# Few changes of the array's form: padded and stacked 64-row operands, values beside scores, and half of the masks on GpSimd, in a top-k attention with a low-rank mixer

## The chip, the core and the metric

The kernel runs on one core of a Trainium2 chip. The core has a matrix engine (TensorE, PE in the profile; its weight loads are shown apart as PEld), a vector engine (VectorE, DVE), an activation engine (ScalarE, ACT), GpSimd (POOL) and SyncE (SP), which here issues the loads. Each works through its own queue of instructions in order; semaphores hold an instruction until what it needs is there. Data lie in SBUF (128 partitions); PE writes to PSUM, from which ACT or DVE copy the results.

The metric is the device time of one execution in microseconds (us), as the median of several runs. A profile is one execution, with every instruction's start and duration.

## The reference

Eight batches of eight heads, 576 positions, 64 features a head. Attention keeps the 32 largest scores of each row; the heads are joined to 512 channels, mixed over the positions by two low-rank factors (rank 32), and passed through an MLP (512 to 2048 to 512). The parameters come as float64.

```python
def _attn_ref(q, k, v) -> np.ndarray:
    B, H, S, D = q.shape
    top_k = 32
    scale = 1.0 / np.sqrt(D)
    scores = scale * np.matmul(q, k.transpose(0, 1, 3, 2))
    kth = np.partition(scores, -top_k, axis=-1)[..., -top_k:-top_k + 1]
    mask = scores >= kth
    scores = np.where(mask, scores, -1000000000.0)
    scores = scores - np.max(scores, axis=-1, keepdims=True)
    attn = np.exp(scores)
    attn = attn / (np.sum(attn, axis=-1, keepdims=True) + 1e-09)
    return np.matmul(attn, v).astype(np.float32)
...
def _moe_ref(x, U, V, w_ch1, w_ch2) -> np.ndarray:
    xt = x.transpose(0, 2, 1)
    h = xt @ U @ V
    u = x + h.transpose(0, 2, 1)
    ch = np.maximum(u @ w_ch1, 0.0) @ w_ch2
    return (u + ch).astype(np.float32)
```

## The kernel before

**Tiling.** The heads go in pairs; one pair of one batch is a *group*, 32 in all. The 576 positions are four blocks of 128 and a tail of 64, so a group has five *steps*. In steps `t` = 0 to 3 DVE works on two tiles of 128 rows by 576 scores, one for each head (two *chunks*); in the last, `t == NT`, on one tile in which the 64 tail rows of both heads lie one above the other. The profile shows the matrix engine's form as rows*columns: `128*128` is the full array; `64*128` has two halves of 64 rows that work side by side (scores, where a head has 64 features); `128*64` and `64*64` have column halves (values: one head to each half of the result). A float32 product is recorded as two passes, a transpose as one.

**One step on DVE.** `front` calls `select`: four times MAX8 (L253, the eight largest), with three MATCH_REPLACE8 between (L262, which takes those eight out), so that the last of the 32 maxima is the threshold. ACT computes the exponentials (L258, with the negative maximum from L257) meanwhile. Then DVE's `scalar_tensor_tensor` (L265) zeroes what lies under the threshold and sums the row into `den`.

**One step on PE.** PE's order is as written by hand; the other engines' instructions are put in order by a scheduler. Step `n` of the loop (L472) issues, in PE's order: the scores of step `n + 1` (L229, copied by ACT at L239 or L242); MLP work; `back` of step `n - 1`, that is the transposes of its masked exponentials E (L300, 128 columns at a time, a part of 64 last, copied by ACT at L301) and at once the product with the values (L307, result `O`, copied at L316 to `XT`); then a piece of `prep` of the next group (transposes of q and k, L207 and L212). In the last step of a group `front` also adds 1e-9 to `den`, takes the reciprocal (L282, L283), and POOL scales E by it (L284).

**Mixing.** When a group's five steps are through, `mixed` transposes `XT` back (L329, L338), DVE scales it by `den` to `X` (L331), and PE makes the two low-rank products (L345, L357), adding `X` by a product with the identity (L360). After every fourth group a batch's `u` is ready, and `mlp` is put on the list of fillers.

**Filling.** `fill` is called between the pieces of a step. A call advances the mixing of a group by one piece, then adds `share` to an account, `due`, and issues MLP work (L382, L400) while the account is above zero. `share` is made so that a batch's MLP takes 160 calls, eight in each of 20 steps. In a two-head step `back` has four pieces, in the last step of a group three, so that step has seven calls.

**Parameters.** In the first 25 steps or so `next_param` loads one or two blocks a step and rounds them from float64 with ACT (L126, L129), POOL (L127, L138) and DVE (L131, L134).

**Buffers.** q and k have two buffers, the score tiles (`Ssb`) three, E six single tiles, PT two, the values three. The PSUM pool of the transposes, `O` and the mixing has two buffers, that of the MLP two, that of the scores two.

Of the kernel before, what the change touches and what calls it, by code (L numbers as in the profile page):

```python
# [21 lines left out]
def kernel(  # L22
# [25 lines left out]

    nc = tc.nc
# [18 lines left out]
    loads = ctx.enter_context(tc.tile_pool(name="loads", bufs=2))  # L68
# [16 lines left out]
    vas = [const.tile([P, 2, NT + 1, D], F32, name=f"va{i}") for i in range(NV)]  # L85
# [56 lines left out]
    def same(a):  # L142
# [5 lines left out]
        ([moe_U[MAIN:S, :]], [(U[0:TAIL, NT, :], same)]),  # L148
# [23 lines left out]
    probs = {}  # L172

    def load(g):
        b, h0 = g // NPAIR, 2 * (g % NPAIR)
        tiles = []
        for name, src in (("q", q), ("k", k)):
            t = loads.tile([P, NT + 1, 2, D], F32, tag=f"ld_{name}", name=f"ld_{name}")
            for i in range(2):
                nc.sync.dma_start(  # L180
                    t[:, 0:NT, i, :],
                    src[b, h0 + i, 0:MAIN, :].rearrange("(p t) d -> p t d", t=NT),
                )
            nc.sync.dma_start(
                t[0:TAIL, NT, :, :], src[b, h0 : h0 + 2, MAIN:S, :].rearrange("h p d -> p h d")
            )
            tiles.append(t)
        va = vas[g % NV]
        for i in range(2):
            nc.sync.dma_start(  # L190
                va[:, i, 0:NT, :],
                v[b, h0 + i, 0:MAIN, :].rearrange("(p t) d -> p t d", t=NT),
            )
        nc.sync.dma_start(
            va[0:TAIL, :, NT, :], v[b, h0 : h0 + 2, MAIN:S, :].rearrange("h p d -> p h d")
        )
        raw[g] = tiles

    def prep(g):

        tiles = raw.pop(g)
# [9 lines left out]
        for i, t in enumerate(tiles):  # L211
            nc.tensor.transpose(  # L212
                tp[:, i, :],
                t[0:TAIL, NT].rearrange("p h d -> p (h d)"),
                ident[0:TAIL, 0:TAIL],
            )
# [3 lines left out]
    def scores(g, t):  # L220
# [4 lines left out]
        S2 = attn.tile([P, 2, S], F32, tag="Ssb", name="Ssb", bufs=3)  # L225
# [10 lines left out]
        for i, sc in enumerate(scs):  # L236
            cs = slice(i * HALF, (i + 1) * HALF)
            if t < NT:
                nc.scalar.copy(S2[:, :, cs], sc[:, :, 0:HALF])  # L239
            else:  # L240
                for h in range(2):
                    nc.scalar.copy(S2[half(h), 0, cs], sc[half(h), h, 0:HALF])  # L242
        S2s[g, t] = [S2[:, 0], S2[:, 1]] if t < NT else [S2[:, 0]]

    def select(chunks, sums):


        Es = [attn.tile([P, S], F32, tag="E", name="E", bufs=6) for _ in chunks]
# [15 lines left out]
        for c in range(len(chunks)):  # L264
            nc.vector.scalar_tensor_tensor(  # L265
                out=Es[c],
                in0=chunks[c],
                scalar=ms[c][:, 7:8],
                in1=Es[c],
                op0=ALU.is_ge,  # L270
                op1=ALU.mult,
                accum_out=sums[c],
            )
        return Es

    def front(g, t):
# [3 lines left out]
        Es = select(chunks, [den[:, 2 * t + h : 2 * t + h + 1] for h in range(len(chunks))])  # L280
        if t == NT:
            nc.vector.tensor_scalar_add(den, den, 1e-9)  # L282
            nc.vector.reciprocal(den, den)  # L283
            nc.gpsimd.tensor_scalar(Es[0], Es[0], den[:, 2 * NT :], None, ALU.mult)  # L284
            del qkTs[g]
        probs[g, t] = Es

    def back(g, t):

        Es, va = probs.pop((g, t)), vas[g % NV]  # L290
        nh = len(Es)
        PT = attn.tile([P, NT + 1, 2, P], F32, tag="PT", name="PT")
        per = 4 // nh
        for j0 in range(0, NT + 1, per):
            js = range(j0, min(j0 + per, NT + 1))
            n = rows(js[0])
            tp = ps_t.tile([P, per, nh, P], F32, tag="tp", name="tp")
            for j in js:
                for h, E in enumerate(Es):
                    nc.tensor.transpose(tp[0 : rows(j), j - j0, h, :], E[:, cols(j)], ident)  # L300
            nc.scalar.copy(PT[0:n, j0 : js[-1] + 1, 0:nh, :], tp[0:n, 0 : len(js)])  # L301
            yield
        m = rows(t)
        O = ps_t.tile([P, P], F32, tag="tp", name="O")
        for j in range(NT + 1):
            for h in range(2):
                nc.tensor.matmul(  # L307
                    O[half(h), 0:m],
                    lhsT=va[0 : rows(j), h, j, :],
                    rhs=PT[0 : rows(j), j, h, :] if nh == 2 else PT[0 : rows(j), j, 0, half(h)],  # L310
                    start=(j == 0),
                    stop=(j == NT),
                )
        if t == 0:
            XTs[g] = attn.tile([P, S], F32, tag="XT", name="XT")
        nc.scalar.copy(XTs[g][:, cols(t)], O[:, 0:m])  # L316
        yield


    def mixed(g):  # L320
# [5 lines left out]
        X = mlpp.tile([P, NT + 1, P], F32, tag="X", name="X")  # L326
# [10 lines left out]
        tp = ps_t.tile([P, P], F32, tag="tp", name="tp")  # L337
        nc.tensor.transpose(tp[0:TAIL, :], XT[:, cols(NT)], ident)  # L338
        nc.scalar.copy(X[0:TAIL, NT, :], tp[0:TAIL, :])
# [3 lines left out]
        for t in range(NT + 1):  # L343
# [3 lines left out]
                lhsT=U[0 : rows(t), t, :],  # L347
                rhs=X[0 : rows(t), t, :],
# [6 lines left out]
        for chunks, (lo, hi) in zip(PARTS, SPAN):  # L355
            up = ps_t.tile([P, WIDE], F32, tag="tp", name="up")
            nc.tensor.matmul(up[:, 0 : hi - lo], lhsT=Tb, rhs=V[:, lo:hi], start=True, stop=False)  # L357
            for t in chunks:
                n = rows(t)
# [167 lines left out]
```

## Time and profile before

| what | us |
|---|---|
| median of 3 runs | 2040.4 (2039.09 to 2041.24) |
| the profiled execution | 2039.95 |
| its span, first to last instruction | 2038.2 |
| ACT busy | 943.8 |
| MAX8, L253 (1152) | 822.2 |
| MATCH_REPLACE8, L262 (864) | 639.2 |
| mask and sum, L265 (288) | 225.0 |
| MLP passes, L382 and L400 (4096) | 1092.2 |
| scores, L229 | 217.4 |
| transposes of E, L300 | 234.1 |
| values, L307 | 234.9 |

Busy times are the union of a group's instructions; matmuls overlap, so that the times of PE's lines say less than the distances between starts. An idle time in a line is the engine's wait just before, with what ended it.

### The profile page before, as it was taken

To read this page: it belongs to the slowest core of one execution; us is meant where nothing else is said; L and a number is where in the kernel's file an instruction comes from. 1 tells how busy PE (TensorE), PEld (TensorE's weight loads), DVE (VectorE), ACT (ScalarE), POOL (GpSimd) and SP (SyncE) were. 2 spreads that over 40 slices of the span, in tenths; PEclk is the share of its full clock that TensorE was granted. 3 is DMA by queue.
4 is the path that set the end of the run, shared out by engine and by line. 5 is a ranking of instruction groups with operands and counts; after the bars stand their busy time and mean duration, and the time that the engine had idled before them with its cause. 6 is when DMAs were issued, how large, how long until landed. Compare 5 with 4: busy or idle time off the path is not lost.

```text
span 2038.2 us, 30289 instructions
## 1 busy us (share of the span) xinstructions
PE 1861.8 (91%) x11424; PEld 1347.3 (66%) x11424; DVE 1740.4 (85%) x3689; ACT 943.8 (46%) x2217; POOL 166.7 (8%) x137
## 2 busy tenths in 40 slices
PE   5666688999999999999999999999999999999998
PEld 3443355677666776677766776667766776667777
DVE  7999999999998999999999999999999999994000
ACT  4555555454544545454544545454554545443111
POOL 2333232000000000000000000000000000000000
PEclk7666689999999999999999999999999999999999
DMA  3222211010001010010000001010000000000000
GB/s 98 69 70 69 74 52 56 18 32 18 23 18 30 8 29 18 19 31 19 27 14 18 22 16 29 18 31 18 28 13 19 19 19 28 1 14 1 11 14 11
DMA packets 98673, 57.21 MB, mean 28 GB/s; under 512 B 83552, under 2 KB 92000, under 8 KB 98528
## 3 DMA queue, kind: packets, MB, share of 16 engines
q1 hardware_dynamic: 95840, 45.85, 8.6%
q0 software_dynamic: 2688, 9.44, 1.2%
q8 instruction: 90, 1.47, 0.3%
q14 instruction: 55, 0.45, 0.1%
HBM read 45.83 MB, written 9.44 MB: 27 GB/s over the span
## 4 chain that ended last, share of the span: by engine, by line
PE 42%; DVE 34%; issue 13%; ACT 7%; DMA 1%; POOL 1%; SPq 1%; POOLq 0%; DVEq 0%; ACTq 0%
DVE m L253 15%; DVE rr L262 14%; PE mm L400 13%; PE mm L382 10%; PE O L307 7%; PE sc L229 5%; DVE E L265 4%; PE tp L300 3%; ACT E L258 2%; ACT PT L301 2%; ACT Ssb L239 2%; DMA raw<-in_moe_w_ch_dram 1%; PE tp L207 1%; PE up L357 1%; PE up L360 1%
## 5 line engine op out<-in xcount | busy, mean ns | idle before, releaser
L253 DVE MAX8 m<-rr 128x8 f32<-128x576 f32 x864 | 615.9, 748 | 2.8
L382 PE MATMUL mm<-uT,w 128*128 128x256 f32 (+1 forms) x2048 | 547.7, 414 | 3.7 <-ACT hT L392 3.7
L400 PE MATMUL mm<-hT,w 128*128 128x256 f32 (+1 forms) x2048 | 544.5, 412 | 0.0
L382 PEld LDWEIGHTS mm<-uT,w 128*128 128x128 f32 x2048 | 374.0, 191 | 122.4 <-issue 32.1
L400 PEld LDWEIGHTS mm<-hT,w 128*128 128x128 f32 x2048 | 372.5, 190 | 115.0 <-issue 29.9
L262 DVE MATCH_REPLACE8 rr<-m,rr 128x576 f32<-128x576 f32 x576 | 427.3, 742 | 0.0
L300 PE MATMUL tp<-ident,E 128*128 128x128 f32 (+1 forms) x1440 | 234.1, 292 | 98.8 <-DVE E L265 54.5
L300 PEld LDWEIGHTS tp<-ident,E 128*128 128x128 f32 (+1 forms) x1440 | 172.5, 142 | 161.3 <-issue 54.6
L253 DVE MAX8 m<-Ssb 128x8 f32<-128x576 f32 x288 | 206.3, 750 | 83.6 <-ACT Ssb L239 80.3
L307 PE MATMUL O<-PT,va 128*64 128x128 f32 (+3 forms) x3200 | 234.9, 286 | 41.7 <-ACT PT L301 38.5
L307 PEld LDWEIGHTS O<-PT,va 128*64 128x64 f32 (+1 forms) x3200 | 170.5, 144 | 118.5 <-ACT PT L301 59.8
L301 ACT COPY PT<-tp 128x512 f32<-128x512 f32 (+1 forms) x448 | 209.2, 496 | 54.2 <-PE tp L300 51.6
L265 DVE SCALAR_TENSOR_TENSOR E<-Ssb,m,E 128x576 f32<-128x576 f32 x288 | 225.0, 813 | 3.2
L258 ACT ACTIVATE E<-Ssb,nmax 128x576 f32<-128x576 f32 x288 | 223.5, 776 | 8.4
L229 PE MATMUL sc<-qkT 64*128 64x288 f32 (+1 forms) x1280 | 217.4, 457 | 1.6 <-ACT Ssb L239 1.6
L392 ACT ACTIVATE hT<-mm 128x320 f32<-128x320 f32 (+1 forms) x256 | 103.7, 406 | 240.9 <-PE mm L382 239.7
L262 DVE MATCH_REPLACE8 rr<-m,Ssb 128x576 f32<-128x576 f32 x288 | 211.9, 742 | 0.0
L239 ACT COPY Ssb<-sc 128x576 f32<-128x576 f32 x256 | 153.0, 641 | 91.3 <-PE sc L229 89.5
L229 PEld LDWEIGHTS sc<-qkT 64*128 64x128 f32 (+1 forms) x1280 | 112.9, 189 | 67.8 <-issue 40.6
L413 DVE TENSOR_TENSOR oT<-uT,mm 128x320 f32<-128x320 f32 (+1 forms) x64 | 28.4, 444 | 150.8 <-PE mm L400 150.6
L257 ACT ACTIVATE nmax<-m 128x1 f32<-128x1 f32 x288 | 57.4, 199 | 200.5 <-DVE m L253 200.4
L284 POOL TENSOR_SCALAR E<-E,den 128x576 f32<-128x576 f32 x32 | 55.4, 1730 | 1122.6 <-DVE den L283 900.9
(53 smaller groups left out, 947.4 us busy)
## 6 DMA issues: line engine op xcount, KB each, us to landing
raw<-in_moe_w_ch_dram SPq DMA_DIRECT2D x32, 512.0 KB, 3.8
ld_q<-in_q_dram SPq DMA_DIRECT2D x64, 128.0 KB, 2.8
ld_k<-in_k_dram SPq DMA_DIRECT2D x64, 128.0 KB, 2.8
va<-in_v_dram SPq DMA_DIRECT2D x64, 128.0 KB, 2.1
out_dram<-ob POOLq DMA_DIRECT2D x16, 512.0 KB, 3.0
ld_q<-in_q_dram SPq DMA_DIRECT2D x32, 32.0 KB, 2.4
ld_k<-in_k_dram SPq DMA_DIRECT2D x32, 32.0 KB, 2.5
va<-in_v_dram SPq DMA_DIRECT2D x32, 32.0 KB, 2.2
```

The lines of the kernel that those rows point to most:

```text
L229: nc.tensor.matmul(sc[slice(0, n) if t < NT else half(h), h, 0:HALF], lhsT=qkT[half(h), 0, cols(t)], rhs=qkT[half(h), 1, i * HALF : (i + 1 ...
L239: nc.scalar.copy(S2[:, :, cs], sc[:, :, 0:HALF])
L253: nc.vector.max(m, curs[c])
L258: nc.scalar.activation(Es[c], chunks[c], AF.Exp, bias=nmax, scale=SCALE)
L262: nc.vector.match_replace(nxt, ms[c], curs[c], NEG)
L265: nc.vector.scalar_tensor_tensor(out=Es[c], in0=chunks[c], scalar=ms[c][:, 7:8], in1=Es[c], op0=ALU.is_ge, op1=ALU.mult, accum_out=sums[c],)
L300: nc.tensor.transpose(tp[0 : rows(j), j - j0, h, :], E[:, cols(j)], ident)
L301: nc.scalar.copy(PT[0:n, j0 : js[-1] + 1, 0:nh, :], tp[0:n, 0 : len(js)])
L307: nc.tensor.matmul(O[half(h), 0:m], lhsT=va[0 : rows(j), h, j, :], rhs=PT[0 : rows(j), j, h, :] if nh == 2 else PT[0 : rows(j), j, 0, half ...
L382: nc.tensor.matmul(ph[:, 0:w], lhsT=w1[:, cc, f * P : (f + 1) * P], rhs=uT[:, cc, lo:hi], start=(cc == 0), stop=(cc == NC - 1),)
L392: nc.scalar.activation(hTs[f][:, 0:w], ph[:, 0:w], AF.Relu)
L400: nc.tensor.matmul(po[:, 0:w], lhsT=w2[:, f, c * P : (c + 1) * P], rhs=hTs[f][:, 0:w], start=(f == 0), stop=(f == NF - 1),)
```

## The change

The tail operands lose their own forms. The two heads' tail rows of q and k are loaded into one tile, `ends`, and transposed once. The tail columns of both heads' E lie side by side, so that one full transpose turns them; the tail values lie on the diagonal of a tile `vd` (zeros elsewhere), so that one full product serves both heads and starts the sum. In the last step of a group the values are one product of the full array for each block (`vt` has zeros above the tail rows), with the result's rows as positions, scaled by `den` on ACT into `X`'s tail; `XT` has no tail to turn back. The tails of `U` and `X` are stacked or padded to 128 rows as well.

`back` is split. `turns` of step `n - 1` (transposes) stays in step `n`; `values` is issued a step later, for `n - 2`, and the scores of `n + 1` right behind it. Every step has eight calls of `fill`, and the loop has one step more.

Of each two-head step the second head's mask is made by POOL (a comparison written over the scores, and a product) with the sum by ACT; in the first four groups all masks are. q and k have one buffer.

```diff
+    ident2 = const.tile([P, TAIL], F32, name="ident2")
+    nc.gpsimd.tensor_tensor(ident2, ident[:, 0:TAIL], ident[:, TAIL:P], ALU.add)
+    vas = [const.tile([P, 2, NT, D], F32, name=f"va{i}") for i in range(NV)]
+    vds = [const.tile([P, P], F32, name=f"vd{i}") for i in range(NV)]
+    vts = [const.tile([P, 2, D], F32, name=f"vt{i}") for i in range(NV)]
+    xs = [const.tile([P, NT + 1, P], F32, name=f"x{i}") for i in range(2)]
...
-    loads = ctx.enter_context(tc.tile_pool(name="loads", bufs=2))
+    loads = ctx.enter_context(tc.tile_pool(name="loads", bufs=1))
...
-        ([moe_U[MAIN:S, :]], [(U[0:TAIL, NT, :], same)]),
+        ([moe_U[MAIN:S, :]] * 2, [(U[:, NT, :], same)]),
...
 def load(g):
+        ends = loads.tile([P, 2, D], F32, tag="ld_ends", name="ld_ends")
...
+                ends[half(len(tiles))], src[b, h0 : h0 + 2, MAIN:S, :].rearrange("h p d -> p h d")
...
+            nc.sync.dma_start(vd[half(i), half(i)], v[b, h0 + i, MAIN:S, :])
+        nc.sync.dma_start(vt[TAIL:P], v[b, h0 : h0 + 2, MAIN:S, :].rearrange("h p d -> p h d"))
...
 def prep(g):
+        nc.tensor.transpose(
+            tp.rearrange("p i n -> p (i n)"), ends.rearrange("p h d -> p (h d)"), ident
+        )
...
 def scores(g, t):
+        main = S2.rearrange("p (h n) -> p h n", h=2)
+        last = S2[:, MAIN : MAIN + 2 * TAIL].rearrange("p (h n) -> p h n", h=2)
+        nc.scalar.copy(main[:, :, 0:HALF], scs[0][:, :, 0:HALF])
+        nc.scalar.copy(main[:, :, HALF:MAIN], scs[1][:, :, 0 : MAIN - HALF])
+        nc.scalar.copy(last, scs[1][:, :, MAIN - HALF : HALF])
...
 def select(chunks, Es, sums, pools):
+            kth = ms[c][:, 7:8]
+            if pools[c]:
+                nc.gpsimd.tensor_scalar(chunks[c], chunks[c], kth, None, ALU.is_ge)
+                nc.gpsimd.tensor_tensor(Es[c], Es[c], chunks[c], ALU.mult)
+                nc.scalar.activation(chunks[c], Es[c], AF.Copy, accum_out=sums[c])
+            else:
+                nc.vector.scalar_tensor_tensor(
...
 def front(g, t):
+        E2 = attn.tile([P, 2 * S], F32, tag="E", name="E", bufs=3)
+        pools = [g < NPAIR or c == 1 for c in range(n)]
...
-            nc.vector.tensor_scalar_add(den, den, 1e-9)
-            nc.vector.reciprocal(den, den)
-            nc.gpsimd.tensor_scalar(Es[0], Es[0], den[:, 2 * NT :], None, ALU.mult)
...
-    def back(g, t):
+    def turns(g, t):
+        E2 = probs.pop((g, t))
+        nh = 2 if t < NT else 1
+        PT = attn.tile([P, 2 * NT + 1, P], F32, tag="PT", name="PT")
+        PTs[g, t] = PT
+        for h in range(nh):
+            tp = ps_t.tile([P, NT, P], F32, tag="tp", name="tp")
+            for j in range(NT):
+                a = h * (S + TAIL) + j * P
+                nc.tensor.transpose(tp[:, j, :], E2[:, a : a + P], ident)
+            nc.scalar.copy(PT[:, NT * h : NT * h + NT], tp)
             yield
+        tp = ps_t.tile([P, P], F32, tag="tp", name="tp")
+        a = MAIN if nh == 2 else S - P
+        nc.tensor.transpose(tp, E2[:, a : a + P], ident)
+        nc.scalar.copy(PT[:, NT * nh], tp)
+        yield
+
+    def values(g, t):
+        PT = PTs.pop((g, t))
+        va, vd, vt = (a[g % NV] for a in (vas, vds, vts))
         O = ps_t.tile([P, P], F32, tag="tp", name="O")
+        if t == NT:
+            den, x = dens[g], xs[g % 2]
+            with tc.high_priority():
+                nc.vector.tensor_scalar_add(den, den, 1e-9)
+                nc.vector.reciprocal(den, den)
+            for j in range(NT + 1):
+                nc.tensor.matmul(
+                    O,
+                    lhsT=PT[:, j],
+                    rhs=va[:, :, j, :] if j < NT else vt,
+                    start=(j == 0),
+                    stop=(j == NT),
+                )
+            for h in range(2):
+                nc.scalar.mul(x[half(h), NT, half(h)], O[half(h), half(h)], den[half(h), 2 * NT :])
+            return
+        nc.tensor.matmul(O, lhsT=vd, rhs=PT[:, 2 * NT], start=True, stop=False)
+        for j in range(NT):
             for h in range(2):
                 nc.tensor.matmul(
+                    O[half(h)],
+                    lhsT=va[:, h, j, :],
+                    rhs=PT[:, NT * h + j],
...
 def mixed(g):
-        tp = ps_t.tile([P, P], F32, tag="tp", name="tp")
-        nc.tensor.transpose(tp[0:TAIL, :], XT[:, cols(NT)], ident)
-        nc.scalar.copy(X[0:TAIL, NT, :], tp[0:TAIL, :])
...
-                lhsT=U[0 : rows(t), t, :],
-                rhs=X[0 : rows(t), t, :],
+                lhsT=U[:, t, :],
+                rhs=X[:, t, :],
...
-                    rhs=ident[0:n, 0:n],
+                    rhs=ident if t < NT else ident2,
...
-    for n in range(STEPS + 1):
+    for n in range(STEPS + 2):
...
             front(g, t)
         for _ in range(1 if 2 <= n < 18 else 2):
             next_param()
+        fill()
+        if n >= 2:
+            values(*divmod(n - 2, CH))
+        if n + 1 < STEPS:
+            scores(*divmod(n + 1, CH))
+        if n >= 2 and (n - 2) % CH == NT:
+            mixing.append(mixed((n - 2) // CH))
         fill(3)
-        if n >= 1:
-            for _ in back(gb, tb):
-                fill()
-            if tb == NT:
-                mixing.append(mixed(gb))
-        if n < STEPS and t >= 1:
-            next(ready, None)
+        if 1 <= n <= STEPS:
+            turning = turns(*divmod(n - 1, CH))
+        next(turning, None)
+        fill()
+        next(ready, None)
+        fill()
+        next(turning, None)
+        fill()
+        next(turning, None)
         fill()
```

## The prediction

> **What bounds the kernel now.** I read the page's totals and slices first, then the busy time by stage, then PE's timeline of one step, then the waits.
>
> ```profile
> PE 1861.8 (91%) x11424; PEld 1347.3 (66%) x11424; DVE 1740.4 (85%) x3689; ACT 943.8 (46%) x2217; POOL 166.7 (8%) x137
> ...
> PE   5666688999999999999999999999999999999998
> ...
> DVE  7999999999998999999999999999999999994000
> ```
>
> By stage (columns: PE, PEld, DVE, ACT, POOL, then PE's granted clock, DMA share, GB/s), and one line of the waits:
>
> ```profile
> 20.00:120.00 100.00, 62.04 (x348) 40.09 (x348) 97.62 (x210) 50.12 (x112) 30.34 (x26) 0.62 0.23 65
> 700.00:900.00 200.00, 195.65 (x1242) 140.03 (x1241) 186.39 (x397) 96.50 (x229) 8.65 (x7) 1.00 0.09 23
> 1850.00:1900.00 50.00, 49.19 (x296) 41.25 (x293) 10.04 (x22) 12.15 (x32) 1.72 (x1) 1.00 0.00 1
> ```
>
> ```profile
> DVE m L253 <- ACT Ssb L239: 80.3, 37, 4.4
> ```
>
> There are three stages. Up to about 315 us (25 steps) DVE is 97% busy and PE 62%, at a clock of 0.62: **DVE sets the pace**. From there to the end of the selections at 1857 us PE is 98% busy and DVE 93%; DVE's idle time is almost all waiting for scores (80.3 us), which PE reaches late: **PE sets the pace** and DVE has some 5% in hand. From 1857 to 2038 PE works alone.
>
> The trace's MAX8 records, in order, give the start of each group (five steps). The first four groups take 57.4, 60.3, 60.4 and 60.2 us, the fifth (MLP beginning, two weight blocks a step) 64.0, the other 27 on average (1857.3 - 315.6) / 27 = 57.1; the rest after 1857.3 is 180.9.
>
> **PE: what a change of form costs.**
>
> ```profile
> 1006.69 2.32 PE L382 MATMUL mm<-uT,w 128*128 128x320 f32 x8
> 1008.94 1.46 PE L307 MATMUL O<-PT,va 128*64 128x128 f32 x20
> 1010.33 1.24 PE L229 MATMUL sc<-qkT 64*128 64x288 f32 x8
> 1011.50 2.42 PE L382 MATMUL mm<-uT,w 128*128 128x320 f32 x8
> 1013.76 0.60 PE L300 MATMUL tp<-ident,E 128*128 128x128 f32 x4
> 1014.20 2.32 PE L382 MATMUL mm<-uT,w 128*128 128x320 f32 x8
> 1016.35 0.27 PE L300 MATMUL tp<-ident,E 128*64 128x128 f32 x1
> 1016.55 1.01 PE L307 MATMUL O<-PT,va 128*64 128x64 f32 x20
> 1017.50 0.66 PE L329 MATMUL tp<-ident,XT 128*128 128x128 f32 x4
> ...
> 1025.00 0.97 PE L360 MATMUL up<-ident,X 128*128 128x128 f32 x6
> 1025.90 0.66 PE L300 MATMUL tp<-ident,E 128*128 128x128 f32 x4
> ```
>
> Compare starts. Eight passes of 320 columns between like forms take 1014.20 to 1016.35 = 2.15 (0.269 each, 0.84 ns a column). Ahead of O they take 2.25: 0.10 more before another form may begin. Behind the scores they take 2.26: 0.11 more, since the first weights can't be loaded ahead. Transposes between units are free of this: 0.44 for four, 0.11 each.
> - O: 20 passes, two side by side, are 10 x 0.108 = 1.08 of columns; the block takes 1.39, so 0.31 inside it is for the first weights, the change to 64*64 for the tail, and the change out. Entered from and left to the full array: 0.10 + 0.31 + 0.11 = 0.52.
> - Scores: four pairs of 288 columns are 0.97, the block takes 1.17. Alone: 0.10 + 0.20 + 0.11 = 0.41.
>
> Together 0.93 a step. After: the tail rows are one full-array product (two passes, 0.22, in place of two pairs, 0.22), the other eight pairs cost the same, and scores follow at once. Left are 0.10 in, 0.05 first weights (half of the 0.11, half as many columns), 0.10 + 0.10 to the scores, 0.09 + 0.11 out: 0.55. That saves 0.38; I take **0.35**, as some blocks stand side by side already (as at 1010.33).
>
> Per group, then:
> - four two-head steps: 4 x 0.35 = 1.4, and 9 transposes for 10: 4 x 0.11 = 0.44
> - last step, O now five padded products of ten full passes: 1.09 against 0.95 (1016.55 to the next block at 1017.50) + 0.10 + 0.11 = 1.16: 0.07
> - L360's tail: six passes took 1025.00 to 1025.90 = 0.90, less 4 x 0.11 = 0.46, + 0.09 behind; padded, two passes of 64 columns are 0.11: about 0.4, I take 0.35
> - first low-rank product: one change fewer, 0.14; q/k tails, one transpose for two in another form, 0.15; XT's tail transpose gone, 0.11
>
> Sum **2.7 us a group**. The five padded products speak for a weighing: the Trainium skill, TensorEngine Tiling (Array Packing), When to Use Tiling, advises tiling wherever a dimension is 64 or less, for up to twice the speed. By that rule the padded O would take twice the 0.95, and 0.9 us a group would be lost instead of 0.07 won; the row above shows why not, since much of that 0.95 is changes and weight loads.
>
> **Filling.** Each step has eight slots of MLP work; the last step of a group had seven, now eight: 40 for 39. The MLP is 4,096 passes of 0.269 or 0.216, 993 us, 31.0 a group at full rate; so a group takes on 31.0/40 = **0.78** more, which leaves the tail.
>
> **Stalls of PE.** My blocks for a group: scores 5 x (0.97 + 0.41) = 6.9, O 4 x (1.08 + 0.52) + 1.16 = 7.6, some 65 transposes (E 45, XT 5, q and k 10, MLP output 5) at 0.11 = 7.2, low-rank products 0.9 + 1.0 + 1.35 = 3.2 (L345, L357, L360 by their starts), MLP 39/40 of 31.0 = 30.2; together 55.1 of 57.1, so 2.0 is waiting, the largest part PE at L307 for the PT copy on ACT (PE's own wait there is 38.5 us in all, 24.6 of it in stalls of over half a microsecond after 450 us). Values come a step later now, so that wait goes: -1.0. New waits (below): bounds 0 and 2; I take +0.5, for a group is mostly PE-bound and its inputs are early.
>
> Steady group: 57.1 - 2.7 + 0.8 - 0.5 = **54.7**; 27 x 2.4 = 65 us saved.
>
> **DVE.** Its free-running step is 1001.97 to 1013.36 = 11.39. One mask less is 0.74 (start to start of the two at L265), so 4 x 10.65 + 6.7 (one-head step) + 1.9 (X, den, oT) = 51.2 a group: below 54.7, so DVE stays in hand and its gain is worth nothing there; it counts only in the first stage: 9 x 0.74 = 6.7 in each of four groups, 3 in the fifth, 30; less what POOL gives back, I take **22**.
>
> **POOL.** A mask is now a comparison (L284's form, 128x576: 1.72), a product of two tensors (not in the trace; nearest L138, 512 wide, 1.27, hence 1.43; bounds 1.27, L138 itself, and 3.4, twice the one-input 1.72; nearest to L138, which also reads two tensors), so 3.15, and a sum on ACT like L258, 0.78 (bounds 0.7 and 1.2). How the two engines meet:
>
> ```profile
> 165.91 0.68 DVE L134 SCALAR_TENSOR_TENSOR bits<-raw,bits 128x512 uint32<-128x512 uint32 x1
> 165.92 2.01 POOL L127 TENSOR_SCALAR size<-size 128x512 f32<-128x512 f32 x1 [10.04 <-ACT size L126]
> ...
> 167.90 1.26 POOL L138 TENSOR_TENSOR w<-bits,low 128x512 uint32<-128x512 uint32 x1
> 168.56 1.22 DVE L265 SCALAR_TENSOR_TENSOR E<-Ssb,m,E 128x576 f32<-128x576 f32 x1
> ```
>
> Beside a two-input instruction of DVE, POOL's comparison is longer by up to 0.5; beside POOL's two-input one, DVE's mask takes 1.22 for 0.81. MAX8 and MATCH_REPLACE8 keep their 0.75 and 0.74 whatever POOL does. In a steady step only POOL's comparison meets DVE's other mask: POOL has E some 3.6 us after the last MAX8, and PE turns it half a step later: hidden. In the first four groups nine masks are 28 us of a 54 us group; weight rounding and L284 were 35.4/110 x 60 = 19 there, so POOL is 85% full, and DVE's rounding (L131, L134) waits behind masks: hence 22 for 30. The Trainium skill, GPSIMD Engine Reference, Engine selection, would keep elementwise work off this engine as about twice slower. By its factor the product would be 1.5; that agrees with the 1.43 and changes no sum, for the engine has room after group five.
>
> **ACT, DMA.** 148 sums of 0.78 are 115 us, and score copies are three for two; ACT goes from 49% to some 60%. Loads are 11 a group for 9, with one buffer instead of two: prep has read it three steps into the group before, so the SP queue doesn't stop: nothing; without that cover one load, about 5 us a group.
>
> **Tail.** MLP work done earlier: 27 x 0.78 = 21. One step more in the pipeline and the last mixing without MLP beside it give back 4 (its four copies, 0.3 to 0.7 each, and their latencies). **-17.**
>
> **Sum.** 2038.2 - 22 - 65 - 17 = 1934, plus 1.8 outside the span (2039.95 - 2038.2): 1936. The profiled execution lies 0.45 below the median, so 1936 it stays.
>
> **Rivals.**
> 1. *ACT stops PE: slower.* ACT works in order, and the sum waits for POOL, 3.6 us after the last MAX8. PT, hT and score copies queue behind it, and PE with its two buffers behind those. For: ACT idles 200 us for DVE's maxima at L257 already. Against: what hides it is that its order can put the sum late, and that it is 40% idle. Whole, it would cost 3.6 x 128 = 460. It decides from (2040 - 1936) / 140 steps = 0.75 a step; at 1.0 a step the time is 1936 + 140 = 2076. Chance 0.13.
> 2. *Narrower window.* Scores stand a slot and a value block (some 2.5 us) later in PE's step, and masks end 3.6 us later, so PE and DVE may drift apart by some 6 us less than before without one waiting. A one-head step alone shifts them by 4 (11.4 - 6.7 on DVE, hardly less work on PE). If each group has 2 us more of waiting, 1936 + 27 x 2 = 1990. Chance 0.17, within it 0.02 for no change.
> 3. *All stalls go.* 57.1 - 2.7 + 0.8 - 2.0 = 53.2, near DVE's 51.2: 27 x 1.5 less, 1895. Chance 0.12.
>
> That the forms don't merge is no rival: nothing is issued between values and scores.
>
> **How the numbers follow.** The forecast, 1936, has 0.58 and its own range is 1905 to 1965. Rival 1 lies above 2040 and is left out of the range, with little at the low end; 1885 to 2005 holds the rest. Within 0.2% (4 us) is about what can't be told from no change. Faster: 0.58 + 0.15 + 0.12 = 0.85; same 0.02; slower 0.13.
>
> **What would show it.** Right: groups near 54.7 us after the fifth; PE's blocks of values and scores adjoining, about 2.5 us together; DVE idle before L253 no less than now; POOL's masks near 3.2 us; no wait at PE for PT. Wrong: PE idle for ACT or POOL before transposes of E; ACT idle for POOL by more than 100 us; or DVE gapless and PE waiting for it.

## The result, and the profile after

The changed kernel takes **2296.64 us** (median of four runs, 2295.25 to 2297.95), the one before 2040.28 beside it (2039.09 to 2041.24): 1.126 times the time, interval 1.124 to 1.128. The forecast was 1936, the range 1885 to 2005; what happened is rival 1, which had 0.13, and the sign named for it, ACT idle for POOL by more than 100 us, is there with 420. The profiled execution's span is 2293.6 us for 2038.2.

The page after, its busy totals and slices, and the shares of the chain of waits:

```profile
PE 1882.4 (82%) x10656; PEld 1406.0 (61%) x10656; DVE 1636.4 (71%) x3393; ACT 1034.5 (45%) x2641; POOL 621.2 (27%) x410
...
PE   4555567998888888888889888888889988898998
...
DVE  6857688777787777787878877788687777887200
...
POOL 5556475221221211222212212122112221222000
...
DVE 41%; POOL 18%; PE 18%; issue 13%; ACT 9%; SPq 0%; DMA 0%; POOLq 0%; DVEq 0%; ACTq 0%
```

PE held a 9 through the steady stage before and now shows mostly 8; DVE fell from 9 to mostly 7. No engine is the bound any more: each has time to spare, so they wait for each other. POOL is half busy in the first slices and 27% in all, and yet has 18% of the chain.

The same three stages as before by windows (columns: PE, PEld, DVE, ACT, POOL, PE's granted clock, DMA share, GB/s):

```profile
20.00:120.00 100.00, 49.20 (x252) 34.19 (x252) 80.94 (x166) 51.97 (x126) 63.39 (x47) 0.62 0.20 55
700.00:900.00 200.00, 172.44 (x1031) 132.09 (x1030) 155.80 (x327) 94.61 (x244) 44.30 (x27) 0.97 0.08 21
2150.00:2200.00 50.00, 50.00 (x217) 37.06 (x217) 1.11 (x2) 9.50 (x24) 0.61 (x1) 1.00 0.03 11
```

In the first stage DVE was 97.62 busy and is 80.94: the engine that set the pace has been relieved of its masks and now idles. In the steady stage PE goes from 195.65 to 172.44 of 200. Only the end, PE alone, is as full as it was.

The waits after (engine, line, what was waited for: us in all, times, longest). L259 copies the scores' tails, L286 is the sum of a POOL mask on ACT, L322 turns E, L323 and L328 copy PT, L352 is the tail product, first in `values`:

```profile
ACT Ssb L286 <- POOL E L285: 420.2, 125, 6.5
DVE m L270 <- ACT Ssb L259: 387.4, 74, 7.3
...
PEld tp L322 <- POOL E L285: 118.6, 30, 8.6
PE tp L322 <- POOL E L285: 102.6, 30, 8.0
...
PE pT L389 <- DVE x L378: 56.4, 31, 2.4
...
PE O L352 <- ACT PT L328: 34.0, 58, 3.7
```

ACT waits 420 us for POOL at the sum, and DVE waits 387 us for score copies on ACT where it waited 80.3. PE's own waits for E from POOL, for X and for PT are smaller, and all of those for POOL's E lie in the first five groups. How the first line makes the second is seen in one step (start, duration, engine, line, [idle before it <- releaser]; of PE's rows only the last is shown):

```profile
1099.75 0.54 ACT L258 COPY Ssb<-sc 128x448 f32<-128x448 f32 x1
1100.01 0.80 DVE L288 SCALAR_TENSOR_TENSOR E<-Ssb,m,E 128x576 f32<-128x576 f32 x1
1100.26 2.14 POOL L284 TENSOR_SCALAR Ssb<-Ssb,m 128x576 f32<-128x576 f32 x1 [21.93 <-DVE m L270]
...
1102.48 1.41 POOL L285 TENSOR_TENSOR E<-E,Ssb 128x576 f32<-128x576 f32 x1
1103.92 0.68 ACT L286 ACTIVATE Ssb<-E 128x576 f32<-128x576 f32 x1 [3.64 <-POOL E L285]
1104.51 0.19 ACT L286 ACTIVATION_READ_ACCUMULATOR Ssb<-E 128x1 f32 x1
1104.60 0.25 ACT L259 COPY Ssb<-sc 128x128 f32<-128x128 f32 x1
1104.88 0.76 DVE L270 MAX8 m<-Ssb 128x8 f32<-128x576 f32 x1 [4.06 <-ACT Ssb L259]
1105.56 0.40 DVE L456 TENSOR_TENSOR oT<-uT,mm 128x256 f32<-128x256 f32 x1
...
1105.78 0.57 ACT L323 COPY PT<-tp 128x512 f32<-128x512 f32 x1
...
1106.11 0.41 PE L468 MATMUL tp<-ident,oT 128*128 128x128 f32 x2 [2.37 <-DVE oT L456]
```

The copies of the next scores are L257, L258 and L259 of the changed kernel. Between L258 and L259 stands the sum of the step before. It waits 3.64 us for POOL's two instructions, and behind it, in ACT's order, wait a copy of 0.25 that ends the scores (DVE stands for 4.06) and, at 1105.78, the PT copy of transposes that PE began at 1101.41 and ended 0.60 later. PE stops too: its next row, a transpose of MLP output, comes at 1106.11 after 2.37 of waiting for oT, which stands behind that MAX8 in DVE's order.

By starts of groups (MAX8 records; the first five counted from the start of the span), the lost time is 368.2 - 315.6 = 52.6 in the first five groups, 27 x (65.34 - 57.10) = 222.5 in the steady ones, and 161.2 - 180.9 = -19.7 behind the last selection; together 255.4, the difference of the spans.

### The profile page after: what moved, and what is told of

It is laid out like the page before. It is cut to its first block, busy times and chain, and to the rows that moved or that the text cites. A ratio compares the mean times of both kernels' runs of the same rounds, so it can differ in the third digit from the quotient of the medians.

```text
span 2293.6 us, 29269 instructions
## 1 busy us (share of the span) xinstructions
PE 1882.4 (82%) x10656; PEld 1406.0 (61%) x10656; DVE 1636.4 (71%) x3393; ACT 1034.5 (45%) x2641; POOL 621.2 (27%) x410
## 4 chain that ended last, share of the span: by engine, by line
DVE 41%; POOL 18%; PE 18%; issue 13%; ACT 9%; SPq 0%; DMA 0%; POOLq 0%; DVEq 0%; ACTq 0%
DVE m L270 21%; DVE rr L279 18%; POOL Ssb L284 10%; POOL E L285 7%; PE mm L425 6%; ACT Ssb L286 3%; PE mm L443 2%; PE O L355 2%; PE sc L239 2%; POOL size L141 1%; ACT Ssb L257 1%; PE tp L322 1%; ACT Ssb L258 1%; ACT E L275 1%; PE up L401 1%
## 5 line engine op out<-in xcount | busy, mean ns | idle before, releaser
L284 POOL TENSOR_SCALAR Ssb<-Ssb,m 128x576 f32<-128x576 f32 x148 | 301.7, 2039 | 1304.5 <-DVE m L270 884.4
L443 PE MATMUL mm<-hT,w 128*128 128x256 f32 (+1 forms) x2048 | 573.4, 429 | 0.0
L322 PE MATMUL tp<-ident,E 128*128 128x128 f32 x1152 | 189.2, 290 | 135.8 <-POOL E L285 102.6
L286 ACT ACTIVATE Ssb<-E 128x576 f32<-128x576 f32 x148 | 101.1, 683 | 421.0 <-POOL E L285 420.2
L322 PEld LDWEIGHTS tp<-ident,E 128*128 128x128 f32 x1152 | 146.0, 149 | 187.6 <-POOL E L285 118.6
L285 POOL TENSOR_TENSOR E<-E,Ssb 128x576 f32<-128x576 f32 x148 | 208.5, 1410 | 11.5
L323 ACT COPY PT<-tp 128x512 f32<-128x512 f32 x288 | 166.7, 579 | 57.8 <-PE tp L322 54.7
L355 PE MATMUL O<-PT,va 128*64 128x128 f32 x2048 | 152.4, 295 | 0.0
L355 PEld LDWEIGHTS O<-PT,va 128*64 128x64 f32 x2048 | 119.3, 146 | 16.9 <-issue 3.1
L364 ACT COPY XT<-O 128x128 f32<-128x128 f32 x128 | 34.0, 266 | 211.4 <-PE O L355 211.4
```

Of the source, the lines that this page charges most:

```text
L284: nc.gpsimd.tensor_scalar(chunks[c], chunks[c], kth, None, ALU.is_ge)
L285: nc.gpsimd.tensor_tensor(Es[c], Es[c], chunks[c], ALU.mult)
L286: nc.scalar.activation(chunks[c], Es[c], AF.Copy, accum_out=sums[c])
L322: nc.tensor.transpose(tp[:, j, :], E2[:, a : a + P], ident)
L323: nc.scalar.copy(PT[:, NT * h : NT * h + NT], tp)
L355: nc.tensor.matmul(O[half(h)], lhsT=va[:, h, j, :], rhs=PT[:, NT * h + j], start=False, stop=(j == NT - 1),)
```

## The experiments

Three theories. **1:** ACT is held by the sums, as above. **2:** the masks on POOL are late in themselves, for whatever needs E. **3:** the new order of the loop costs PE its time, whoever makes masks.

All of them beside the kernel before (2040.44, 2041.38 and 2039.68 us beside a to d, e to h, and j to m). The columns by group are from the traces: first five groups, then the mean of the other 27, then what follows the last selection. "Split" is PE's time by starts, a group, for groups 6 to 29 (counted from 0): columns at 0.842 ns, and what a matmul takes above that, in gaps up to 0.45 us ("small": changes of form, first weights, but also short stalls and a lower clock, see the last section) and in longer ones (waits).

| kernel | us | ratio, 95% | first five | steady | rest | split: columns + small + waits |
|---|---|---|---|---|---|---|
| before | 2040 | 1 | 315.6 | 57.10 | 180.9 | 49.44 + 5.41 + 2.43 |
| after | 2296.64 | 1.126 (1.124 to 1.128) | 368.2 | 65.34 | 161.2 | 50.14 + 5.79 + 9.77 |
| a: all masks on DVE | 2048.99 | 1.004 (1.002 to 1.005) | 313.4 | 58.40 | 156.7 | 50.16 + 4.29 + 4.15 |
| b: sums later | 2048.58 | 1.004 (1.003 to 1.005) | 338.3 | 57.44 | 157.8 | 50.15 + 4.02 + 3.37 |
| c: POOL masks in before | 2335.95 | 1.145 (1.142 to 1.147) | 374.0 | 65.96 | 182.7 | 49.55 + 8.29 + 8.50 |
| d: after without sums | 2042.38 | 1.001 (1.000 to 1.002) | 329.1 | 57.54 | 157.8 | 50.14 + 4.08 + 3.33 |
| e: b, scores first | 2014.31 | 0.987 (0.985 to 0.988) | 337.0 | 56.10 | 158.8 | 50.14 + 4.52 + 1.63 |
| f: b, mixing later | 2047.86 | 1.003 (1.002 to 1.005) | 363.0 | 56.32 | 162.5 | 50.16 + 3.64 + 2.71 |
| g: b, DVE masks at first | 2022.34 | 0.991 (0.989 to 0.992) | 311.0 | 57.47 | 157.7 | 50.15 + 4.11 + 3.37 |
| h: b + e + f + g | 1995.35 | 0.978 (0.976 to 0.979) | 306.2 | 56.45 | 163.9 | 50.16 + 4.50 + 1.91 |
| j: b + e + g, tail product last | 1981.45 | 0.971 (0.970 to 0.973) | 313.0 | 55.91 | 158.5 | 50.14 + 3.94 + 2.01 |
| k: j, all masks on DVE | 2019.96 | 0.991 (0.988 to 0.993) | 314.6 | 57.26 | 157.0 | 50.14 + 4.67 + 2.58 |
| l: a in before's loop | 2052.6 | 1.006 (1.004 to 1.008) | 315.6 | 57.67 | 181.0 | 49.34 + 4.61 + 3.80 |
| m: j, one slot more in mixing | **1966.4** | 0.964 (0.962 to 0.965) | 308.8 | 55.40 | 160.1 | 50.16 + 3.78 + 1.66 |

### What stopped the kernel: a, b, c, d

**a.** The masks go back to DVE, forms and order stay as changed.

```diff
-        pools = [g < NPAIR or c == 1 for c in range(n)]
+        pools = [False] * n
```

> The changed kernel with every mask and sum back on the vector engine (nothing on POOL, no sums on ACT); forms, order and filling stay as changed. Theory 1 (ACT is held by the sum that waits for POOL): the loss goes whole, and the form part alone shows: PE's 2.7 us a group, DVE nearly the bound at 54 us a group, about 1980 us (1940 to 2020). Theory 2 (E comes late from POOL and holds PE's transposes): the same, 1980. Theory 3 (scores behind values leave DVE and PE too narrow a window): the loss stays for the most part, above 2150.

2048.99: all but 9 us of the loss comes with the masks on POOL; theories 1 and 2 both say so. Also, forms and order without POOL masks do not win: waits are 4.15 a group for 2.43.

**b.** The edit moves nothing but the sum in ACT's order: behind the last PT copy of the same step. Masks stay on POOL. PE's 10656 matmuls stay in the same order; the scheduler places some of the others anew, but 2025 of ACT's other 2345 instructions keep theirs.

```diff
-                nc.scalar.activation(chunks[c], Es[c], AF.Copy, accum_out=sums[c])
+                late.append((chunks[c], Es[c], sums[c]))
...
-        nc.scalar.copy(PT[:, NT * nh], tp)
+        turned = nc.scalar.copy(PT[:, NT * nh], tp)
+        with tc.issue_after(turned.ins):
+            for chunk, E, total in sums_of.pop((g, t)):
+                nc.scalar.activation(chunk, E, AF.Copy, accum_out=total)
```

> The changed kernel with the same work on the same engines; only ACT's order differs: each sum of a POOL mask is queued behind the last PT copy of the same step, so that ACT meets it when POOL has long finished. Theory 1: the loss goes, about 1940 us (1900 to 2000), ACT idle for POOL near 0 instead of 420 us. Theory 2: the loss stays, above 2200, with PE waiting for POOL's product as before (220 us on both of its queues) or more. Theory 3: above 2200.

2048.58: **248 us come back from where the sums stand in one engine's order**. The line of the sum in b, with its instructions (duration in ns, min/median/max, first and last start), its waits and who waits for it:

```profile
L333 ACT ACTIVATE Ssb<-E x148: 677/696/712, 33.0 to 1897.2; 128x576 f32<-128x576 f32 x148
L333 ACT ACTIVATION_READ_ACCUMULATOR Ssb<-E x148: 192/202/218, 33.6 to 1897.7; 128x1 f32 x148
its engine sat idle before it (us, times) until:
who waited for it (us, times):
  DVE den L344: 17.6, 5
```

The same 148 sums, as long as before, and no wait ahead of any: 420.2 us have become none. Its price is 17.6 us in all, where a group's last sums are needed for the denominators. That settles theory 1 against 2 for the steady groups: POOL takes as long in b as it did (2.13 and 1.41 for a mask at 1108.60), and PE's direct waits for its E, 102.6 us after and 100.4 in b, lie in the first five groups in both.

**c.** The kernel before, with its forms and its order; the second head's masks, and all in the first four groups, made by POOL with the sum where the changed kernel issues it.

```diff
+            kth = ms[c][:, 7:8]
+            if pools[c]:
+                nc.gpsimd.tensor_scalar(chunks[c], chunks[c], kth, None, ALU.is_ge)
+                nc.gpsimd.tensor_tensor(Es[c], Es[c], chunks[c], ALU.mult)
+                nc.scalar.activation(chunks[c], Es[c], AF.Copy, accum_out=sums[c])
...
+                    [g < NPAIR or h == 1 for h in range(len(chunks))])
```

> The kernel before with one thing of the change: the second head's mask (all masks in the first four groups) made by POOL with the sum on ACT; forms and order of before. Theory 1: slower than before, 2150 to 2350, ACT idle for POOL by some hundreds of us. Theory 2: slower too, 2100 to 2300, the wait being PE's at the transposes of E, which come earlier here than in the changed kernel. Theory 3: near before, 1990 to 2050.

Its waits:

```profile
ACT Ssb L269 <- POOL E L268: 370.6, 135, 6.6
DVE m L253 <- ACT Ssb L239: 313.1, 66, 9.0
```

2335.95, with the same two lines on top: the fault needs neither the new forms nor the new order.

**d.** The changed kernel without the sums; the denominators are set to 1, so the rows of E that were to be summed aren't normalised.

```diff
-                nc.scalar.activation(chunks[c], Es[c], AF.Copy, accum_out=sums[c])
...
+            nc.vector.memset(dens[g], 1.0)
```

> The changed kernel without the sums of the POOL masks (their den entries stay 1, so the normalisation of these rows is left out); POOL makes the masks as in the change. Theory 1: the loss goes, about 1930 us (1890 to 1990). Theory 2: hardly anything changes, above 2200. Theory 3: above 2200.

2042.38, and 57.54 a group against b's 57.44: in the right place, the sums cost a steady group nothing; what d gains on b (6 us) lies in the first five groups (9 us). But a, b and d end 29, 49 and 52 us above the ranges that theory 1 gave them: with the sums out of the way, the gain is missing too.

### What stood in the way of the gain: e, f, g, h

With the sums out of the way, b still lies 113 us above the forecast. Three waits are left in its trace; each of the next kernels takes one away. The first is the tail product (L357) behind the copy of the last transpose (L330), some 1 us a group; the second pT (L394) behind X (L383); the third is E turned (L324) behind POOL. In b's waits:

```profile
PE tp L324 <- POOL E L287: 100.4, 33, 6.5
...
PEld O L357 <- ACT PT L330: 57.9, 58, 5.0
...
PE O L357 <- ACT PT L330: 36.2, 58, 4.6
PE pT L394 <- DVE x L383: 35.7, 23, 3.3
```

The first of the four lines has the same 100.4 us and 33 times in a list cut off at 300 us: it lies in the first stage alone.

**e.** Scores ahead of values in the step, on b.

```diff
-        if n >= 2:
-            values(*divmod(n - 2, CH))
         if n + 1 < STEPS:
             scores(*divmod(n + 1, CH))
+        if n >= 2:
+            values(*divmod(n - 2, CH))
```

> The late-sums kernel (2048.6 us; a steady group is 57.5: 50.2 of columns, 4.0 of form changes and weight loads, 3.4 of PE waiting) with one more edit: in each step the scores are issued before the values instead of behind them, still side by side. Theory W (what the forms save goes into waits that the new order makes at certain places): the wait between the last transpose of E and the tail product, 0.99 us a group for the PT copy, is covered by the scores; 27 groups x 0.9 = 25 less, 2024 (2010 to 2035). Theory C (PE and DVE hold one another in turn, so that a wait removed in one place comes up in another): 2040 to 2055.

2014.31. PE's timeline of a step in b, then in e:

```profile
1141.60 1.89 PE L430 MATMUL mm<-uT,w 128*128 128x256 f32 x8
1143.33 0.38 PE L357 MATMUL O<-PT,vd 128*128 128x128 f32 x2
1143.64 1.09 PE L360 MATMUL O<-PT,va 128*64 128x128 f32 x16
1144.66 1.24 PE L239 MATMUL sc<-qkT 64*128 64x288 f32 x8
1145.83 1.99 PE L430 MATMUL mm<-uT,w 128*128 128x256 f32 x8
```

```profile
1133.23 1.24 PE L239 MATMUL sc<-qkT 64*128 64x288 f32 x8
1134.40 0.49 PE L357 MATMUL O<-PT,vd 128*128 128x128 f32 x2
1134.82 1.09 PE L360 MATMUL O<-PT,va 128*64 128x128 f32 x16
1135.84 1.99 PE L430 MATMUL mm<-uT,w 128*128 128x256 f32 x8
```

By starts, the tail product takes 0.31 in b (a full-array product behind a full-array one) and 0.42 in e, where it is one more change of form. The order that changes form less is the slower one: e pays 0.50 a group more in "small" (0.85 at full clock, last section) and loses 1.74 of waits, since the PT copy has the scores' time to land.

**f.** The work of a finished group (`mixed`) is made ready at the end of the step instead of ahead of its slots, so that its pT comes later behind X.

```diff
-        if n >= 2 and (n - 2) % CH == NT:
-            mixing.append(mixed((n - 2) // CH))
         fill(3)
...
         next(turning, None)
+        if n >= 2 and (n - 2) % CH == NT:
+            mixing.append(mixed((n - 2) // CH))
         fill()
```

> The late-sums kernel with one more edit: the mixing of a group enters the list at the end of the step, as before the change, so that the scores of the next step and MLP work lie between turning XT back and the low-rank product. Theory W: the waits for X ahead of that product, 0.88 + 0.24 + 0.19 = 1.3 us a group, go; 27 x 1.2 = 32 less, 2017 (2005 to 2035). Theory C: 2040 to 2055.

2047.86, not to be told from b. The steady groups are 1.1 us shorter: by starts, the wait for X fell from 1.30 to 0.18 a group, but a new one of 0.88 came up where XT is turned back (L381), for a PT copy, as theory C has it. The first five are 25 us longer; PE's waits for POOL's E, all of them there, are 121.5 for 100.4. In h, where DVE makes these masks, the 25 are gone; how the place of the mixing lengthens them stays open.

**g.** In the first four groups all masks on DVE, as before; from the fifth on, the second head's on POOL.

```diff
-        pools = [g < NPAIR or c == 1 for c in range(n)]
+        pools = [g >= NPAIR and c == 1 for c in range(n)]
```

> The late-sums kernel with one more edit: in the first four groups all masks are DVE's (with every mask there the groups took 57 to 61 us with DVE's masks throughout, 63 to 67 with POOL's). If POOL, full with masks and weight rounding, holds these groups, they go back to 57 to 61: 20 to 25 less, 2026 (2015 to 2035). If the late sums or the forms hold them, they stay at 63 to 67 and the time at 2049.

2022.34, 26 us less than b; the first five groups are 27 shorter: POOL masks there are a loss, with the sums in the right place too. Windows of the first stage, b and then g, and DVE's longest wait in b's:

```profile
20.00:120.00 100.00, 54.27 (x280) 37.31 (x278) 84.80 (x168) 56.56 (x136) 68.75 (x51) 0.59 0.23 67
```

```profile
20.00:120.00 100.00, 60.84 (x316) 41.88 (x314) 97.54 (x211) 51.92 (x121) 28.21 (x25) 0.62 0.24 67
```

```profile
DVE bits L145 <- POOL size L141: 10.5, 3, 5.8
```

In b DVE is 84.80 busy with 168 instructions, in g 97.54 with 211: relieving DVE put PE behind POOL (the 100.4 us above), and DVE too, which idles 15.2 us here, 10.5 of them for POOL's part of the weight rounding.

**h.** e, f and g together on b.

> The late-sums kernel with the three edits together (scores before values, mixing later, first four groups on DVE). Theory W: the gains add up, 25 + 32 + 22, 1970 us (1950 to 2000), steady groups near 55.3. Theory C: only the first groups gain, 2015 to 2035, steady groups still 57 or more.

1995.35: 53 us below b, where the three apart gave 34, 1 and 26. That they fall short of their sum by only 8 is in part luck. In the steady groups the three gave 2.4 us a group apart and give 0.99 together, 39 us less over 27 groups; f's edit on top of e's makes these groups 0.35 longer (56.45 for 56.10), and its new wait at L381 is there with 0.55. The first five groups, where f's 25 us are gone, give 28 more than the three apart.

### A version that beats both: j, k, l, m

**j.** e and g on b, with the tail product last in `values` instead of first, so that the PT copied last is needed last.

```diff
-        nc.tensor.matmul(O, lhsT=vd, rhs=PT[:, 2 * NT], start=True, stop=False)
...
-                    start=False,
-                    stop=(j == NT - 1),
+                    start=(j == 0),
+                    stop=False,
...
+        nc.tensor.matmul(O, lhsT=vd, rhs=PT[:, 2 * NT], start=False, stop=True)
```

> Late sums, scores before values, all masks of the first four groups on DVE, and the tail product issued last in the values instead of first: behind the scores it had cost one change of form more (scores to full array to column halves; 20 changes a group in the trace of scores-first against 16 in late sums). Scores-first was 2014.3 us; the first groups give 26 (2048.6 to 2022.3 with that edit alone) and four changes a group at 0.1 give 27 x 0.45 = 12: 1976 us (1965 to 1990). If the waits come up elsewhere instead (theory C): 1985 to 2010.

1981.45. The full-array product now stands ahead of MLP passes of the same form, and "small" is back at 3.94 a group, 0.58 less than in e; waits are 0.38 more. So the steady groups gain 0.19 on e, 5 us in all where 12 were expected.

**k.** j with every mask on DVE (`pools = [False] * n`).

> The same kernel with every mask on DVE. If the masks on POOL are worth something once ACT isn't held by them, this is slower than tail-last: DVE needs some 54 us a group instead of 51, close to PE's, and a group becomes about 1 us longer as between all-DVE masks and late sums (58.6 against 57.5): 2003 us (1990 to 2025). If POOL's masks are only a burden: 1976 or less.

2019.96: 38 us more than j, 27 x (57.26 - 55.91) = 36 of it in the steady groups. So **the masks on POOL are worth having once nothing queues behind them**, though PE sets the pace there. Waits are 0.57 a group longer in k and "small" 0.73, though PE has the same matmuls; most of the 0.73 is PE's clock (last section).

**l.** The forms of a in the loop of before: scores at the head of the step, values right behind the transposes, seven slots in a group's last step.

```diff
+            if n + 1 < STEPS:
+                scores(*divmod(n + 1, CH))
...
+            for _ in turns(gb, tb):
+                fill()
+            values(gb, tb)
+            fill()
```

> The changed forms (stacked and padded tails) with every mask on DVE and the loop's order of before: scores first, values right behind the transposes of the same step, mixing at the end of the step, seven slots in a group's last step. If the forms alone carry a gain and the new order took it back: a steady group of 55.8 for 57.3 (some nine changes fewer at 0.1, four transposes fewer at 0.11, products the same), 27 x 1.5 = 40 less, 2000 us (1985 to 2020). If DVE and PE hold one another so that PE's work does not count: 2030 to 2045.

2052.6, no better than a, and above both ranges. In its waits:

```profile
PE O L352 <- ACT PT L328: 66.7, 83, 4.2
```

With the tail product first and values right behind the turning, PE waits for the PT copied last, 38.5 us of such waits before and 66.7 now. With DVE's masks, then, neither loop gains by the new forms. The rest behind the last selection is 181.0, as before, and the columns a group are back at 49.34: that fits the eighth slot as what shortens the end, though l changes the loop's order too.

**m.** j with one empty slot more between X and pT (`yield` once more in `mixed`).

> Tail-last with one empty piece more in the mixing, so that a slot of MLP work more lies between turning XT back and the low-rank product, which waited for X 1.2 us a group. Theory W: 27 x 0.8 = 20 less than tail-last, about 1955 us. Theory C: within 8 us of tail-last.

**1966.4**, 0.964 of before (0.962 to 0.965), the fastest of all; 15 us less than j, of 20 expected. Its totals and slices:

```profile
PE 1785.4 (91%) x10656; PEld 1343.5 (68%) x10656; DVE 1649.0 (84%) x3465; ACT 1027.0 (52%) x2569; POOL 511.4 (26%) x338
...
PE   4556578999999999999999999999999999999998
...
DVE  7999999988889989888889989888899998887000
```

The 9s are back on PE with the same 10656 matmuls as after, and DVE shows the relief that the masks on POOL were to bring.

## Why the prediction was wrong

**What bounds the kernel** stands: DVE first, PE then, PE alone at the end. So do the prices of POOL and ACT: product 1.43, measured 1.41; comparison 1.72 and up to 0.5 more beside DVE's mask, measured 1.73 alone and 2.14 beside it; the sum 0.78, measured 0.68 + 0.19 = 0.87.

**The step that failed** is in the stalls: "New waits (below): bounds 0 and 2; I take +0.5, for a group is mostly PE-bound and its inputs are early". It goes with the sentence that set rival 1 aside: "what hides it is that its order can put the sum late, and that it is 40% idle". The waits of a steady group rose by 9.77 - 2.43 = 7.3 instead of falling by 0.5. That the order *could* put the sum late says nothing of where it stands; in ACT's order it stood ahead of copies that PE and DVE needed. An engine that is idle 40% of the time is no cover either, because what is held is not its time but its queue. Rival 1's whole price was 460; the place of the sum is worth 248 (after less b), 1.8 us a step for the 0.75 from which it decides.

**The first stage** was -22 and is +52.6; +22.7 remain with the sums moved (b). The weak point was there in the numbers: "POOL is 85% full". "PE turns it half a step later: hidden" was worked out for a steady step with one mask on POOL. With two of 3.5 us in a row and rounding between them, PE waits 100 us for E there. The term was right in what DVE is spared and in the wait it named ("DVE's rounding (L131, L134) waits behind masks"), but it took 8 us for that, 30 less 22: in b DVE idles 15.2 us of the 100 shown (2.4 before), and POOL, 69% busy as the stage grows longer, is what both others wait for.

**The forms** were right as a mechanism, and the term 2.7 mis-sized. Values and scores adjoin and take 1145.83 - 1143.33 = 2.50 us where some 2.5 were named, and what is left of the changes in that step is 0.55 as worked out: 0.09 at the tail product (0.31 less 0.22), 0.16 at the heads (1.02 less 0.86), 0.20 at the scores (1.17 less 0.97), 0.10 behind them. But in the whole group "small" fell by 5.41 - 4.02 = 1.4 (b), and columns, less the MLP's share, by 0.15: about 1.5. Recorded changes of form fell from 36.2 to 18.0 a group. Of b's 4.02, 0.50 lies in stretches of half clock (last section), of before's 5.41 only 0.07; without these the fall is 1.8, 0.10 a change, and the whole some 2.0. Where the other 0.7 of the 2.7 went wasn't worked out by block. That the blocks stood alone before, on which the sum rests, is so: values and scores adjoin in 6 of the 120 steps of groups 6 to 29.

**The stalls taken away:** the -1.0 for values behind PT did not come either, though the wait was there before with 1.07 a group by starts (the 24.6 us given as a part of PE's own 38.5 are those of the weight loads, of 59.8 in all). The new order put the tail product first in `values`, and its PT is the one copied last: 1 us a group in b. With pT behind X, waits were +0.9 a group in b; e and j show that scores first and the tail product last get that back (-0.4 in j).

**Filling** was +0.78 and is +0.87 of MLP columns. **The tail** was -17 and is -19.7 (after) and -23.1 (b); l, without the eighth slot, has none of it. The single buffers of q and k cost what was said, nothing: L220 waits 5.5 us in all for loads after, 83.2 for ACT.

**DVE's gain** in the steady groups, "worth nothing there", was wrong in the other direction: k against j makes it 1.35 a group, with the forms and the order of j.

Put together for b: +22.7 + 27 x 0.34 - 23.1 = +8.8 against before, where -22 - 65 - 17 was predicted. Even with the sums late the forecast would have missed. m ends 30 us above it: steady groups are 55.40 for 54.7 (19 us more), the first five groups give 6.8 for 22 (15 more), and the end is 3.8 shorter than was said.

Not shown are why the sums were issued where they were (only the order is seen in the trace), where 0.7 of the forms' 2.7 went, and how f's place of the mixing costs 25 us.

## What to carry to other kernels

An instruction that waits for a slow engine holds everything behind it in its own engine's order, however idle that engine is: before work is split over two engines, write down what stands behind the joining instruction, and place that instruction behind the copies that others need. Fewer changes of form were worth 0.1 us each from before to b and 0.2 from e to b (0.85 for 3.8 changes a group), less than one wait of a product for the operand copied last; issue a product of that operand last, and put other work ahead of it. Relief for the engine that sets the pace is relief only if the engine that takes the work over returns it before the next one needs it: a stage in which that engine was reckoned 85% full, and was 69% busy, is not such a place. A wait taken away is a gain only if it doesn't come up elsewhere, as f's did.

## What was not expected of the hardware

Stalls cost PE more than their own length. In the trace after:

```profile
1121.84 1.12 PE L220 MATMUL tp<-ident,ld_q 128*128 128x128 f32 x4 [3.10 <-ACT PT L323]
1122.74 1.06 PE L401 MATMUL up<-V,Tb 128*128 128x256 f32 x2
```

Behind a wait of 3.10 us four transposes take 1.12 where other blocks of four take 0.60, and two passes of 256 columns 1.06 for 0.70 in j. The granted clock shows why (windows as above, PE first, the clock third from the end):

```profile
1118.21:1121.62 3.41, 0.53 (x6) 0.39 (x4) 3.41 (x7) 1.95 (x5) 1.39 (x1) 1.00 0.00 0
1121.63:1125.04 3.41, 3.21 (x12) 2.67 (x12) 3.34 (x9) 2.17 (x6) 0.00 (x0) 0.50 0.15 35
```

In the 3.41 us in which PE was busy for 0.53 the clock was full; in the 3.41 behind them it is half. In groups 6 to 29, half clock takes 4.27 us a group after, 6.68 in c, 1.99 in k, 1.14 in b, 0.71 in j, 0.14 before, and none in m. Of "small", 2.21 lies in such stretches after, 3.28 in c, 0.94 in k, 0.50 in b, 0.34 in j, 0.15 in e, 0.07 before. Without them after and b, which have the same matmuls in the same order, are at 3.58 and 3.52, and c and before, with the old forms, at 5.01 and 5.34. So the waits behind the sums cost PE some 1.7 us a group on top of their own length. The Trainium skill (TensorE: Matmul & The Clock Gate, What's actually happening) has the clock halved after an idle window of about 3.4 us that runs freely; the lengths fit it, though the window seen here was not wholly idle.

When POOL's comparison and DVE's mask of the same step run together, the one that starts second is the longer. After, DVE's mask started first in 104 such pairs: the comparison took 2.14 for 1.73, the mask 0.80, no longer than alone. In 9 the comparison started first: it took 1.72, and the mask 1.02. The Trainium skill (GPSIMD Engine Reference, Specifications) names contention with DVE's instructions of two inputs. And the sum on ACT is two instructions, 0.68 and 0.19 for reading the accumulator, in each of 148.
